# Attention into experts: routing's pieces a step later, the choice's sums on TensorE, a written order for the last four units, and the first weights around the first gather

## The chip, the cores and the metric

One core of a Trainium2 chip runs the whole program. The metric is the device time of one execution in microseconds; the time given for a kernel is the median of its runs. An execution's span runs from its first to its last instruction in the trace and is a little shorter than its time.

## What is computed

The reference, cut to what matters:

```python
# attention: 4 batches, 8 heads, 576 tokens, head size 64; fp32
scores = scale * q @ k.T + slopes * (-abs(rel))
scores = where((rel >= 0) & (rel < 128), scores, -1e9)
attn = softmax(scores)                       # each row over at most 128 keys
x = (attn @ v).reshape(2304, 512)            # 2304 tokens
# experts: 8, one per token
logits = x @ w_gate + modality_bias[modality_id]
e = argmax(logits); gate = softmax(logits)[e]
x = gate * (relu(x @ w1[e]) @ w2[e])         # 512 -> 1024 -> 512
# a dense layer
h = x @ w_in                                 # 512 -> 2048
out = (h * cos(h)) @ w_out
```

## The kernel before

**Attention.** The 2304 tokens are 18 tiles of 128 (t), in two pairs of batches (bp, nine tiles each). A unit n is one tile and one group of four heads (hg), so there are 36 units, n = 2t + hg. One step of the loop starts the scores of unit n (`score`: 12 products into bank S, then masks and the row maximum on VectorE and the exponentials on ScalarE), turns the probabilities e of unit n-2 (`flip`: transposes into bank P, a copy on ScalarE, two masks on GpSimd; units 8, 9, 26 and 27 have three key blocks and three groups of transposes, the second of them in bank T), turns q and k of a unit to come (`tr`: transposes of rqk into bank T), and forms the weighted sum of unit n-3 (`pv`: bk<-vt,pT into bank O, then den, its reciprocal and the scaling on VectorE, lines 769 to 773). Banks in this stage: S three, T two, P, O and L one each. An fp32 product is issued as two matmuls, a transpose as one.

**Routing** is woven into the same loop. When both units of a tile are summed, the tile X[t] (xt, or y for the last two) goes to `x_dram` and `later` enters its pieces under a step and a half (0 or 1) of it: `xt_split` (four transposes into bank T, a copy on ScalarE, line 803, and the rest on VectorE, line 804), and for every second tile `products` (eight products xT by wg into bank L, copied to ls), `choose` (two transposes of ls into bank L, two additions and six more operations on VectorE, the one-hot oh) and `ranks` (seven bf16 products and a dozen operations on VectorE). `setups(i)` runs setup calls twice a step: the tables all at i = 8, the modality's bias with a transpose of mf in bank T at i = 13.

**Order.** TensorE's and GpSimd's instructions keep the written order while `Turns.on` holds, from step 2 to 33; else, and on VectorE and ScalarE always, a planner orders them by its own costs. SyncE issues the loads and stores in its queue's order.

**The seam.** Tiles 0 to 15 (TE = 16) fill the first item of 256 token slots. After their ranks, `early` picks the expert with most tokens (`first`), multiplies the one-hots (`second`: ob by oa0, 16 products into bank L), gets the row indices idx0, gathers the 256 rows of `x_dram` in two halves of 128 rows (`gather(0)`, an indirect transfer issued by GpSimd into xg0 and xg1), and loads that expert's first weights: w1 in pieces of 512 KB (`load_w1`, with the expert's number read from regs by SyncE) and w2 (`load_w2`). `order` compares the experts' keys for the later plan. Behind that come the tail's units and tiles 16 and 17, whose stores stand behind the first piece of w2 (`MK["w"]`).

**Experts and after.** Nine items and the rest of 128-row blocks: each item turns its gathered rows (`to_xT`), multiplies by w1 and w2 split into two fp32r parts (casts to s on ScalarE, the rest on VectorE), and stores y. The rows of the items from the second on come from the full table (`late`: sums, slots, table on VectorE, 18 products on TensorE), which needs the ranks of tile 17. Then the dense layer, from about 435 us.

## Time and profile before

| | |
|---|---|
| median of 3 runs | 843.32 us (842.28 to 845.54) |
| the profiled execution | 844.73 us |
| its span | 843.0 us |
| TensorE busy, share of the span | 801.4 us, 95% |
| VectorE | 614.7 us, 73% |
| ScalarE | 492.1 us, 58% |
| GpSimd | 201.2 us, 24% |
| mean granted clock of TensorE | 0.989 |

How to read it: a busy time is the sum of an engine's instructions in the profiled execution; matmuls are pipelined and their ends modelled, so a following instruction may start before the shown end. The granted clock is the share of TensorE's full 2.4 GHz that the chip let through; 0.50 is 1.2 GHz. In a timeline a row is one instruction or several alike in a row, with start, time, engine, line, operation, written tile and read tiles, shapes and count; in brackets stands how long the engine was idle before it and what ended that. Lines 494 and 1079 are helpers that record many operations, so there the tile names tell them apart.

### The profile page before, as it was taken

To read this page: it belongs to the slowest core of one execution; us is meant where nothing else is said; L and a number is where in the kernel's file an instruction comes from. 1 tells how busy PE (TensorE), PEld (TensorE's weight loads), DVE (VectorE), ACT (ScalarE), POOL (GpSimd) and SP (SyncE) were. 2 spreads that over 40 slices of the span, in tenths; PEclk is the share of its full clock that TensorE was granted. 3 is DMA by queue.
4 is the path that set the end of the run, shared out by engine and by line. 5 is a ranking of instruction groups with operands and counts; after the bars stand their busy time and mean duration, and the time that the engine had idled before them with its cause. 6 is when DMAs were issued, how large, how long until landed. Compare 5 with 4: busy or idle time off the path is not lost. (4 is left out here: it accounts for less than half of the span.)

```text
span 843.0 us, 14736 instructions
## 1 busy us (share of the span) xinstructions
PE 801.4 (95%) x5269; PEld 705.8 (84%) x5269; DVE 614.7 (73%) x1463; ACT 492.1 (58%) x912; POOL 201.2 (24%) x259
## 2 busy tenths in 40 slices
PE   7899999979899999999999999999999999999996
PEld 5789888969799999999878778787788888888995
DVE  3866686668889999996749989896665555555562
ACT  6675677534557576664637676764554454444562
POOL 5655565510122132230001121112212001100100
PEclk9899999989999999999999999999999999999999
DMA  8555441044788888869433232501312001100000
GB/s 158 141 143 126 120 120 38 28 148 141 260 278 273 273 284 278 267 221 335 158 125 100 80 106 73 176 25 51 112 38 75 1 1 37 38 1 0 26 26 25
DMA packets 125134, 103.40 MB, mean 123 GB/s; under 512 B 61725, under 2 KB 105027, under 8 KB 125059
## 3 DMA queue, kind: packets, MB, share of 16 engines
q1 hardware_dynamic: 122099, 92.74, 36.3%
q0 software_dynamic: 2960, 9.70, 3.2%
q8 instruction: 42, 0.69, 0.3%
q14 instruction: 33, 0.27, 0.1%
HBM read 85.90 MB, written 16.52 MB: 121 GB/s over the span
## 5 line engine op out<-in xcount | busy, mean ns | idle before, releaser
L1079 PE MATMUL bk<-hh,s 128*128 128x256 f32 x864 | 117.7, 284 | 7.8 <-DVE y L1079 4.6
L1079 PEld LDWEIGHTS bk<-hh,s 128*128 128x128 f32 x864 | 107.8, 188 | 10.1 <-DVE y L1079 5.6
L1079 PE MATMUL bk<-xT,s 128*128 128x256 f32 x864 | 114.5, 282 | 1.7 <-DVE s L1079 1.1
L1079 POOL TENSOR_TENSOR lf<-lf,mag 128x512 f32<-128x512 f32 x32 | 46.9, 1467 | 282.1 <-DVE mag L1079 246.9
L1079 PEld LDWEIGHTS bk<-xT,s 128*128 128x128 f32 x864 | 107.4, 188 | 2.2 <-DVE s L1079 1.3
L1079 ACT CAST s<-r 128x1024 fp32r<-128x1024 f32 x72 | 75.2, 1050 | 54.4 <-DMA r<-in_moe_w_dram 40.4
L1079 PE MATMUL bk<-yT,wi_a 128*128 128x512 f32 (+1 forms) x480 | 104.4, 368 | 1.2 <-DVE yT L1079 0.8
L1079 PE MATMUL bk<-yT,wi_b 128*128 128x512 f32 (+1 forms) x480 | 105.0, 368 | 0.0
L1079 DVE TENSOR_TENSOR s<-r,s 128x1024 fp32r<-128x1024 f32 x72 | 94.3, 1313 | 13.6 <-ACT s L1079 13.2
L1079 ACT ACTIVATE r<-r 128x512 f32<-128x512 f32 (+1 forms) x80 | 47.2, 590 | 92.5 <-DVE r L1079 92.5
L1079 PEld LDWEIGHTS bk<-yT,wi_a 128*128 128x128 f32 x480 | 84.0, 188 | 17.3 <-DVE yT L1079 1.1
L1079 PEld LDWEIGHTS bk<-yT,wi_b 128*128 128x128 f32 x480 | 84.6, 188 | 15.7
L1079 DVE TENSOR_TENSOR r<-bk,r 128x512 f32<-128x512 f32 (+1 forms) x80 | 50.9, 636 | 62.1 <-ACT r L1079 61.4
L1079 PE MATMUL bk<-wo_b,gg 128*128 128x512 f32 x384 | 93.7, 391 | 2.5 <-DVE po L1079 1.1
L1079 PE MATMUL bk<-wo_a,gg 128*128 128x512 f32 x384 | 92.8, 390 | 0.6 <-DVE gg L1079 0.5
L1079 PEld LDWEIGHTS bk<-wo_b,gg 128*128 128x128 f32 x384 | 71.4, 188 | 19.7 <-ACT o L1079 1.5
L1079 PEld LDWEIGHTS bk<-wo_a,gg 128*128 128x128 f32 x384 | 71.8, 188 | 16.5 <-DVE gg L1079 1.5
L1079 DVE TENSOR_TENSOR gg<-r,gg 128x512 fp32r<-128x512 f32 x64 | 46.1, 720 | 34.3 <-ACT gg L1079 34.3
L494 PE MATMUL bk<-vt,pT 128*128 128x65 f32 x544 | 66.8, 276 | 0.1
L494 PEld LDWEIGHTS bk<-vt,pT 128*128 128x128 f32 x544 | 65.1, 195 | 1.2 <-issue 1.0
L1079 ACT CAST gg<-r 128x512 fp32r<-128x512 f32 x64 | 39.7, 620 | 41.1 <-DVE r L1079 40.2
L1079 DVE SCALAR_TENSOR_TENSOR r<-ki,bk 128x512 f32<-128x512 int32 (+1 forms) x80 | 50.4, 630 | 16.5 <-ACT ki L1079 15.9
(280 smaller groups left out, 1279.5 us busy)
## 6 DMA issues: line engine op xcount, KB each, us to landing
r<-in_moe_w_dram SPq DMA_DIRECT2D x72, 512.0 KB
y_dram<-y SPq DMA_DIRECT2D x19, 256.0 KB
rqk<-in_q_dram SPq DMA_DIRECT2D x32, 128.0 KB
rqk<-in_k_dram SPq DMA_DIRECT2D x32, 128.0 KB
vt<-in_v_dram SPq DMA_DIRECT2D x32, 128.0 KB
x_dram<-xt SPq DMA_DIRECT2D x16, 256.0 KB
f64x<-in_moe_w_in_dram SPq DMA_DIRECT2D x8, 512.0 KB
raw<-in_moe_w_dram SPq DMA_DIRECT2D x8, 512.0 KB
```

Of the source, the lines that this page charges most:

```text
L494: self.last = op(*args, **kwargs)
L1079: r = op(*args, **kwargs)
```

## The change

- `xt_split` is entered under half 1 of its step instead of half 0, `products`, `choose` and `ranks` under half 0 of the three steps behind. The calls of half 1 now come before the weighted sum.
- `choose` forms the logits in PSUM: the bias enters by a product of ident with biasm, and the two halves of ls (hi and lo weights) are summed by a product with both, a matrix of two stacked identities. The two transposes and VectorE's two additions go. The last comparison writes ohb before oh.
- The tables' setup is called one at a time from i = 8 on; `setup_route` is cut into three parts at i = 13, 14 and 15, with its transpose in bank L.
- All groups of `flip` use bank P; a weighted sum is cut after two heads, and the further groups of `flip` come in between and behind.
- The loop ends two steps sooner, and the last units' calls are written out one by one; `Turns.on` holds to the end. In this order the scaling of units 33 and 34, the masks of unit 35 and the key of `order` stand behind idx0. Sums of units 33 and 35 use bank S.
- `second` issues w1's first piece ahead of the gather; then half of the gather, a copy of the expert's number to reg0 on GpSimd, the other half, a read of reg0 on SyncE, w1's second piece and w2's first.

```diff
@@ -207,6 +207,7 @@
...
     idx = rt.tile([128, NBLK], I32, name="idx")
+    reg0 = rt.tile([1, 1], I32, name="reg0")
...
@@ -282,16 +283,22 @@
...
                 nc.tensor.matmul(tp, ob[:, t], oa0[:, t], start=t == 0, stop=t == TE - 1)
-            V_.tensor_scalar(idx0, tp, float(NT // 2), None, op0=ALU.add)
-            gather(0)
-
+            MK["idx0"] = V_.tensor_scalar(idx0, tp, float(NT // 2), None, op0=ALU.add)
             load_w1(0, 0)
+            first_rows = gather(0, 0)
+
+
+            with tc.issue_after(first_rows.ins):
+                nc.gpsimd.tensor_copy(reg0, regs[:, 2 * NL + 1:2 * NL + 2])
+            gather(0, 1)
+            EV[0] = nc.sync.value_load(reg0[0:1, 0:1], min_val=0, max_val=NE - 1)
             load_w1(0, 1)
...
             key = rt.tile([128, NE], F32, name="key")
-            V_.scalar_tensor_tensor(key, eo, -2.0 * NE, iota[:, 0:NE], op0=ALU.mult, op1=ALU.add)
+            with tc.issue_after(MK["idx0"].ins):
+                V_.scalar_tensor_tensor(key, eo, -2.0 * NE, iota[:, 0:NE], op0=ALU.mult, op1=ALU.add)
             shp = [128, NE, NE]
...
@@ -460,11 +467,13 @@
...
     def gather(i, u=None):
-        for j in range(2 if u is None else 1):
+        for j in range(2) if u is None else [u if i == 0 else 0]:
             ap = idx0[:, j:j + 1] if i == 0 else idx[:, 2 * i + j:2 * i + j + 1] if u is None else \
                 idx[:, 2 * MIN_ITEMS + u:2 * MIN_ITEMS + u + 1]
-            nc.gpsimd.indirect_dma_start(out=xgs[j], out_offset=None, in_=x_dram[0:128 * TE if i == 0 else NT, :],
-                                         in_offset=bass.IndirectOffsetOnAxis(ap=ap, axis=0))
+            ins = nc.gpsimd.indirect_dma_start(
+                out=xgs[j], out_offset=None, in_=x_dram[0:128 * TE if i == 0 else NT, :],
+                in_offset=bass.IndirectOffsetOnAxis(ap=ap, axis=0))
+        return ins
...
@@ -556,6 +565,7 @@
...
         wg = rt.tile([128, KD, 2, NE], F32R, name="wg")
+        both = rt.tile([2 * NE, NE], F32, name="both")
         wr = ca.tile([128, KD, NE], F32, name="wr")
...
@@ -576,15 +586,18 @@
...
             nc.vector.tensor_tensor(wg[:, :, 1], wr, wg[:, :, 0].bitcast(F32), op=ALU.subtract)
+            nc.vector.tensor_tensor(both, ident[:2 * NE, 0:NE], ident[:2 * NE, NE:2 * NE], op=ALU.add)
             mf = ca.tile([T, 128], F32, name="mf")
             nc.vector.tensor_copy(mf, mi.rearrange("t (p two) -> t p two", two=2)[:, :, 0])
-            mp = bank("T", [128, T])
+            yield
+            mp = bank("L", [128, T])
             nc.tensor.transpose(mp, mf, ident[:T, :T])
...
                     nc.vector.tensor_copy(md[:, 9 * bp + s:9 * bp + s + 1], mp[:, 9 * bp + 13 - s:9 * bp + 14 - s])
+            yield
             m0 = ca.tile([128, T], F32, name="m0")
...
@@ -711,6 +724,8 @@
...
                 products(sc, pairs)
+                if n == N - 1:
+                    yield
                 for j in range(2):
...
@@ -735,9 +750,9 @@
...
             for g in (0, 4, 8) if nv == 3 else (0,):
-                if g == 8:
+                if g:
                     yield
-                pp = bank("P" if g != 4 else "T", [128, 4, 128])
+                pp = bank("P", [128, 4, 128])
                 for c in range(4):
...
@@ -759,13 +774,17 @@
...
             heads, t0 = PT.pop(n)
-            ot = bank("O", [128, 4, 128])
+            ot = bank("S" if n >= END and n % 2 else "O", [128, 4, 128])
             for h, pT in enumerate(heads):
+                if h == 2:
+                    yield
                 for b in range(len(pT)):
...
             den = sm.tile([128, 4], F32, name="den")
+            if n > END:
+                yield
             nc.vector.tensor_scalar(den, ot[:, :, D], 1.0e-9, None, op0=ALU.add)
...
@@ -780,15 +799,15 @@
...
                 if t < TE - 2:
-                    later(p, 0, lambda: xt_split(t))
+                    later(p, 1, lambda: xt_split(t))
                 else:
...
                     if t < TE - 2:
-                        later(p, 1, calls[0])
-                        later(p + 1, 0, calls[1])
-                        later(p + 2, 1, calls[2])
+                        later(p + 1, 0, calls[0])
+                        later(p + 2, 0, calls[1])
+                        later(p + 3, 0, calls[2])
                     else:
...
@@ -817,25 +836,22 @@
...
             def choose():
-                lt = bank("L", [128, 2, 2, NE])
+                lg = bank("L", [128, 2, NE])
+                nc.tensor.matmul(lg, ident, biasm[:, t:t + 2], start=True, stop=False)
                 for j in range(2):
-                    nc.tensor.transpose(lt[:, j].rearrange("p a e -> p (a e)"), ls[:, 128 * j:128 * j + 128],
-                                        ident[:2 * NE, :2 * NE])
+                    nc.tensor.matmul(lg[:, j], ls[:, 128 * j:128 * j + 128], both, start=False, stop=j == 1)
                 shp = [128, 2, NE]
-                lg = rt.tile(shp, F32, name="lg")
                 mx = rt.tile([128, 2], F32, name="lmx")
...
                 rv = rev.unsqueeze(1).to_broadcast(shp)
-                nc.vector.tensor_tensor(lg, lt[:, :, 0], biasm[:, t:t + 2], op=ALU.add)
-                nc.vector.tensor_tensor(lg, lt[:, :, 1], lg, op=ALU.add)
                 nc.vector.tensor_reduce(mx, lg, op=ALU.max, axis=AX.X)
...
                 nc.vector.tensor_reduce(m2, o, op=ALU.max, axis=AX.X)
-                nc.vector.tensor_tensor(o, rv, m2.unsqueeze(2).to_broadcast(shp), op=ALU.is_equal)
-                MK["oh"] = nc.vector.tensor_tensor(ohb, rv, m2.unsqueeze(2).to_broadcast(shp), op=ALU.is_equal)
+                nc.vector.tensor_tensor(ohb, rv, m2.unsqueeze(2).to_broadcast(shp), op=ALU.is_equal)
+                MK["oh"] = nc.vector.tensor_tensor(o, rv, m2.unsqueeze(2).to_broadcast(shp), op=ALU.is_equal)
...
@@ -876,11 +892,10 @@
...
                     todo.extend(LATER.pop())
-                if i == 8:
-                    for fn in tables:
-                        fn()
-                if i == 13:
-                    setup_route()
+                if i >= 8 and tables:
+                    tables.pop(0)()
+                if i >= 13:
+                    next(route, None)
                 for fn in todo[:1 if i > 1 else 2]:
...
@@ -892,41 +907,73 @@
...
-        LATER = []
+        LATER, route = [], setup_route()
         END = N - 4
-        turned = [n + LF for n in range(N)]
-        summed = [n + LP for n in range(N)]
-        for n in range(END - 2, N):
+        turned = [n + LF for n in range(END + 1)]
+        summed = [n + LP for n in range(END)]
+        for n in range(END - 2, END + 1):
             turned[n] = max(n + 1, END)
-            summed[n] = max(n + 2, END + 1)
-        for n in range(N + 2):
+            if n < END:
+                summed[n] = END + 1
+        for n in range(END + 2):
             if n < 3:
                 ahead(n, dt=n + 1)
-            Turns.on = 1 < n <= END + 1
-            scores = score(n) if n < N else iter(())
+            Turns.on = n > 1
+            scores = score(n)
             next(scores, None)
...
             calls(due.pop((n, 0), []))
-            if n > END:
-                calls([after.pop(0) for _ in after[:2]])
-            flips = [flip(m) for m in range(N) if turned[m] == n]
+            calls(after)
+            flips = [flip(m) for m in range(END + 1) if turned[m] == n]
             for p in flips[:1]:
...
             setups(2 * n + 1)
-            sums = [m for m in range(N) if summed[m] == n]
-            for m in sums[:1]:
-                pv(m)
-            for p in flips:
+            calls(due.pop((n, 1), []))
+            sums = [pv(m) for m in range(END) if summed[m] == n]
+            for p in sums[:1]:
+                next(p)
+                for f in flips:
+                    next(f, None)
                 run(p)
-            for m in sums[1:]:
-                pv(m)
-            calls(due.pop((n, 1), []))
-            if n > END:
-                calls([after.pop(0) for _ in after[:2 if n < N + 1 else 1]])
+            for f in flips:
+                run(f)
+            for p in sums[1:]:
+                run(p)
+
+        split15, logits14, choice14, ranks14, slots0, rows0, order0 = after
+        after.clear()
+        run(score(N - 2))
+        calls(due.pop((END + 2, 0)))
         assert not due
+        split15()
+        run(flip(N - 3))
+        sum32 = pv(END)
+        next(sum32)
+        logits14()
+        run(sum32)
+        choice14()
+        score35 = score(N - 1)
+        next(score35)
+        run(flip(N - 2))
+        ranks14()
+        sum33, sum34, sum35 = (pv(n) for n in range(END + 1, N))
+        for p in (sum33, sum34):
+            next(p)
+            next(p)
+        slots0()
+        rows0()
+        with tc.issue_after(MK["idx0"].ins):
+            run(sum34)
+            run(sum33)
+            run(score35)
+        order0()
+        after.pop(0)()
+        run(flip(N - 1))
+        run(sum35)
+        after.pop(0)()
...
```

## Rows read from the trace of the kernel before

**Rows 1.** Busy time by engine, clock, DMA share and GB/s in four stretches.
```profile
core 0: us, PE busy (x) PEld busy (x) DVE busy (x) ACT busy (x) POOL busy (x), PEclk, DMA share, GB/s
20.00:160.00 140.00, 132.23 (x1232) 119.26 (x1233) 99.83 (x506) 94.78 (x242) 81.88 (x136) 0.98 0.43 106
28.00:32.00 4.00, 3.69 (x19) 3.70 (x20) 2.35 (x12) 2.72 (x8) 2.52 (x4) 0.57 0.95 221
38.00:42.00 4.00, 4.00 (x27) 3.71 (x27) 3.54 (x16) 0.92 (x2) 1.50 (x3) 0.58 0.34 101
182.00:192.00 10.00, 6.83 (x30) 4.81 (x29) 4.60 (x7) 3.70 (x6) 2.13 (x2) 0.50 1.00 349
```

**Rows 2.** Groups by form on TensorE, 20 to 178 us.
```profile
line engine op names shapes xcount | busy us, mean ns | idle before us <-releasers
L494 PE MATMUL bk<-vt,pT 128*128 128x65 f32 x528 | 64.0, 274 | 0.0
...
L494 PE MATMUL bk<-ident,rqk 128*128 128x128 f32 x116 | 18.6, 283 | 2.5 <-DVE xT L804 1.8 <-DMA rqk<-in_q_dram 0.5 <-DMA rqk<-in_k_dram 0.2
L494 PE MATMUL bk<-ident,xt 128*128 128x128 f32 x64 | 12.6, 307 | 3.6 <-DVE xt L773 3.5
L494 PE MATMUL bk<-xT,wg 128*16 128x256 f32 x64 | 9.3, 282 | 0.3 <-DVE xT L804 0.3
...
L494 PE MATMUL bk<-ident,mf 18*128 18x18 f32 x1 | 0.2, 203 | 1.3 <-DVE mf L580 1.3
```

**Rows 3.** TensorE's timeline in the loop: the longest gap that routing makes.
```profile
28.31 0.67 PE L494 MATMUL bk<-ident,xt 128*128 128x128 f32 x2 [1.70 <-DVE xt L773]
```

**Rows 4.** TensorE's timeline at the seam, 165 to 194 us.
```profile
165.94 0.97 PE L494 MATMUL bk<-kT,qT 64*128 64x256 f32 x12
166.84 0.44 PE L494 MATMUL bk<-ident,e 128*128 128x128 f32 x2
167.12 1.90 PE L494 MATMUL bk<-vt,pT 128*128 128x65 f32 x16
168.85 0.17 PE L494 MATMUL bk<-ohb,tri 128*128 128x8 bf16 x1
168.88 0.17 PE L494 MATMUL bk<-cum,ones 128*128 128x8 bf16 x1
...
181.19 0.55 PE L494 MATMUL bk<-oa,ob 128*128 128x2 f16 x16 [1.92 <-DVE oa L279]
...
188.97 1.12 PE L1079 MATMUL bk<-ident,xg 128*128 128x128 f32 x4 [2.00 <-DMA xg<-x_dram,idx]
...
190.73 1.05 PE L1079 MATMUL bk<-ident,xg 128*128 128x128 f32 x4
...
193.19 1.22 PE L1079 MATMUL bk<-xT,s 128*128 128x256 f32 x8 [0.22 <-DVE xT L1079]
```

**Rows 5.** TensorE's timeline at a choice, and what follows it.
```profile
159.29 0.29 PE L494 MATMUL bk<-ident,ls 16*128 16x16 f32 x2
159.51 0.66 PE L494 MATMUL bk<-ident,e 128*128 128x128 f32 x4
```

**Rows 6.** VectorE's timeline at the seam, 177 to 187 us.
```profile
177.85 0.16 DVE L214 TENSOR_TENSOR fold<-bk,oh 128x16 f32<-128x16 f32 x1
...
179.09 0.69 DVE L804 TENSOR_TENSOR xT<-bk,xT 128x512 fp32r<-128x512 f32 x1
...
184.52 1.23 DVE L1079 TENSOR_TENSOR s<-r,s 128x1024 fp32r<-128x1024 f32 x1
```

**Rows 7.** GpSimd's timeline: issues of the gathers, 180 to 215 us.
```profile
182.23 1.16 POOL L494 DMA_INDIRECT xg<-x_dram,idx  x1 [10.38 <-DVE idx L285]
183.69 0.97 POOL L494 DMA_INDIRECT xg<-x_dram,idx  x1 [0.30 <-issue]
209.08 1.06 POOL L1079 DMA_INDIRECT xg<-x_dram,idx  x1 [24.42 <-DVE nu L364]
```

**Rows 8.** DMA queues (packets, MB, share): first 184 to 186.5, then 187 to 189 us.
```profile
q1 hardware_dynamic: 411, 0.66, 84.9%
q0 software_dynamic: 2, 0.01, 2.3%
...
q0 software_dynamic: 143, 0.47, 59.5%
```

**Rows 9.** TensorE's timeline where the second item's rows are awaited.
```profile
212.65 0.66 PE L1079 MATMUL bk<-ident,xg 128*128 128x128 f32 x4 [0.88 <-DMA xg<-x_dram,idx]
```

## The prediction

> **What bounds the kernel now.** I began with the chain of waits and the busy shares: the chain is a chain of TensorE products from some 435 us on, and the change touches nothing there, so what it can bring is an earlier arrival at that stage. I then read TensorE's idle time stage by stage. In the attention loop, from 20 to 160 us, TensorE is busy for 132.2 of 140.0 us at a mean clock of 0.98 [rows 1]: it is the bound, and a gap in it is lost time. The groups by form say whose gaps they are: 3.5 us before the transposes of xt and 0.3 us before the logits' products, 1.8 us before the transposes of rqk (they want the bank that the token tile's split still holds, so the releaser is xT of line 804), and 1.3 us before the transposes of the modality's mf [rows 2]. All four belong to routing, 6.9 us in all. The largest, 1.70 us, ends at 28.31 [rows 3]. The granted clock in 28 to 32 us is 0.57 and in 38 to 42 us 0.58 [rows 1], so TensorE spent most of these stretches at 1.2 instead of 2.4 GHz, behind the holes of line 804's tile and of mf.
>
> The second place is the seam between attention and experts. Between 182 and 192 us the clock is 0.50 throughout, and TensorE is busy for 6.8 of 10 us even so [rows 1]. The order of TensorE's instructions shows why: the products that turn the first tokens' places into indices (oa, ob) wait 1.92 us for VectorE, then the transposes of the gathered rows wait 2.00 us for the gather, and the first expert products run freely from 193.19 [rows 4].
>
> All of this is measured in an execution that took 844.73 us (843.0 us of it the span), 1.41 us above the median of 843.32. I sum savings against 844.73 and take the same savings off the median.
>
> **The change part by part: the loop.** (a) The routing's pieces come later. The transposes of a finished tile move from right behind the scores to ahead of the weighted sum, still in the same step; logits, choice and ranks move up to one step each. The setup of the tables is cut into single calls and that of the modality into three. No work is added; 6.9 us of gaps should go. What is late next? The steps with three key blocks now put all three groups of transposes through bank P, which has one buffer, with half of a weighted sum between two groups. Sixteen products of a weighted sum take 1.73 us (167.12 to 168.85 [rows 4]), so half, of the usual size, covers 0.87 us, and a copy out of the bank has to fit into that and the transposes of rqk beside it. There are four such steps; two of them now wait for the bank of line 804, 1.8 us in all [rows 2]. I take 0.2 us each, 0.8 us in all, between 0 and 3.6.
>
> (b) The clock. The lost share is (1 - 0.57) x 4 + (1 - 0.58) x 4 = 3.4 us of full speed. If the two holes go, the work behind them runs at 2.4 GHz, and I take the 3.4 us as gained; the bounds are 0 and 3.4. Against it: 0.7 us of waiting for q and k stands in the same groups [rows 2] and stays.
>
> (c) The choice on TensorE. Two transposes become three fp32 products, and an fp32 product is issued as two matmuls here: the weighted sums count 528 for 264 [rows 2]. So six matmuls with 128 weight columns replace two instructions that take 0.22 us (159.29 to 159.51 [rows 5]). No row has fp32 matmuls with 8 or 16 moving columns. From above, an fp32 matmul of the weighted sum follows the one before it after 0.108 us (1.73 / 16 [rows 4]), with 65 columns; from below, the bf16 matmuls of the ranks, with 8 columns, follow after 0.03 us (168.85 to 168.88 [rows 4]). Type decides, I think, since the two instructions on ls, fp32 with 16 columns, also cost 0.11 each. So 6 x 0.108 = 0.65 us, 0.43 more than now. Seven rounds lie in the loop: 3.0 us lost; the bounds are a gain of 0.3 and, if each matmul costs 0.2 us, a loss of 6.9. VectorE's two additions go, but VectorE is busy for 99.8 of 140 us there [rows 1] and this saves nothing by itself. The Trainium skill (TensorE: Matmul & The Clock Gate, section Back-to-back issue gap) gives about 81 ns for a pair of weight load and matmul in a stream at 128 columns; by that the rounds would cost 1.1 us less. The trace's 0.108 us for fp32 is larger, and the measurement decides.
>
> Loop: 6.9 - 0.8 + 3.4 - 3.0 = 6.5 us.
>
> **The seam: up to the indices.** Before, the weighted sum of unit 31 ends at 168.85, after the scores of 34 and two transposes that the planner put ahead of it (1.18 us, 165.94 to 167.12); the index products begin at 181.19, 12.34 us later [rows 4]. In the written order that 1.18 us moves behind the sum. Of the 12.34 us, 1.92 was waiting; the eight transposes of tile 16 and of unit 35 move behind the index (0.14 us each by the pair at 166.84 [rows 4], 1.1 us), the 1.18 us move in, and one choice costs 0.43 more: 12.34 - 1.92 - 1.1 + 1.18 + 0.43 = 10.9 us, from a start 1.18 us sooner. Together 2.6 us sooner, if TensorE does not wait. VectorE's chain from ranks to index products ran from 177.85 to 181.19; the split that stood in it at 179.09 took 0.69 us [rows 6] and lies elsewhere in the new order; the key and its comparison, and the last units' scaling, are put behind idx0. So about 2.6 us remain of 3.3, and the weighted sums of 33 and 34 (24 matmuls, 2.6 us) stand in front of it. For the joint, and the choice's chain before it, I leave 0.4 us: 2.2 us gained. Bounds: 0.5 and 3.0.
>
> **The seam: from the indices to the first products.** Before: 181.19 to 193.19, 12.0 us. GpSimd starts the gather 1.04 us in, and the second half 1.46 us later [rows 7]. Ahead of them on SyncE's queue stood two pieces of w1, one of w2 and a store. In 184 to 186.5 us the gather's queue moved 0.01 MB and SyncE's 0.66; the gather's 0.47 MB came in 187 to 189 [rows 8], and the transposes started at 188.97, 6.74 us after the issue. A later gather with nothing ahead of it is awaited until 212.65, 3.57 us after its issue at 209.08 [rows 7, 9]. The new order issues w1's first piece, then half the gather, then a one-element copy on GpSimd, then the other half; SyncE reads that copy before it issues w1's second piece, w2's first and the stores queued behind them. The copy has no row; between 0 and the 0.97 us of a gather's issue, I take 0.4. The second half is then issued 1.04 + 1.46 + 0.4 = 2.9 us in, takes 3.6 us, and 0.7 more for sharing with w1's piece: 7.2 us. From the second half's transposes to the first products it took 2.46 us before (190.73 to 193.19): 9.7 us instead of 12.0. What hides the late second piece: issued some 3 us in, with the gather's 3.6 us and 1.5 for its half megabyte at 349 GB/s [rows 1], it lands some 8 us in; two conversions of 1.23 us [rows 6] end at 10.6, and it is wanted 24 products after the first, at about 12.3. Without that margin TensorE would wait in its place. One such conversion may fall into VectorE's routing chain, since the earlier window for it closes; I charge half, 0.6. 12.0 - 9.7 - 0.6 = 1.7 us. Bounds: -1 and 3.
>
> By the Trainium skill (DMA: Bandwidth & Descriptors, section Queues, rings and completion order) an engine takes turns between the queues that have work, packet by packet, so that a gather would not stand behind a backlog; the rows here show it standing. What follows if the rule holds all the same is rival C.
>
> **Sum.** 6.5 + 2.2 + 1.7 = 10.4 us: 834.3 in the profiled execution's terms, **832.9 us** for the median. The expert stage behind it is shifted as a whole: its weights are loaded as buffers come free, and those come free earlier too.
>
> **The rivals.**
> A. *The gaps in the loop change their name.* The transposes wait for bank P or for q and k instead of for routing, and the clock still falls. For it: q and k are awaited for 0.7 us already [rows 2]. Against it: most of a step now lies between each producer and its reader. At the upper bound of the new waits and without the clock the loop gives 6.9 - 3.6 - 3.0 = 0.3, and with the seam's 3.9 that is 4.2: 839.1.
> B. *The written tail makes the last tile late.* The last unit's masks, exponentials, transposes and sum now all follow idx0, on four engines in turn, at half the clock. If products of tile 17 end 2.5 us later than I reckon, ranks and the full table are late, and the second item waits for its tokens, as it already does for 0.88 us at 212.65 [rows 9]. The second part of the seam then loses 1 us instead of gaining 1.7: 6.5 + 2.2 - 1.0 = 7.7: 835.6.
> C. *Holding back w1 buys nothing*, because the gather's delay was not the backlog. The second part of the seam gives 0: 8.7 saved, 834.6. Against it: the gather's packets came only when SyncE's queue thinned out [rows 8]. By the rule of the Trainium skill cited above (DMA: Bandwidth & Descriptors) this would be the outcome.
> D. *Slower: the choice opens holes.* Each of its six matmuls shows its whole latency, 274 ns as the mean of such a one [rows 2], because each adds to the same bank: 1.64 us instead of 0.22, and a hole of that size was followed by a stretch at the low clock that cost 1.7 us [rows 1, 3]. Seven rounds cost 7 x (1.42 + 1.7) = 21.8; against 6.1 of gaps, 3.4 of clock and 1.5 left of the seam, 10.8 slower: 854.1. It decides from about 1.6 us a round, hole and clock together. Against it: the weighted sums add to one bank too and follow at 0.108 us.
>
> **How the numbers follow.** A measurement of this kernel can tell about 0.5%, 4.2 us, from no change. Forecast 0.46, all faster. A 0.18, which straddles that bound: 0.07 faster, 0.11 within. B 0.13: 0.08 and 0.05. C 0.10: 0.09 and 0.01. D 0.13, slower. Together 0.70, 0.17, 0.13. The low end takes the cheap bound of the choice and no new waits: 832.9 - 3.3 - 0.8 - 1.8 = 827.0. The high end is A with the choice at 0.2 us a matmul, 3.9 more, 843.0, of which I leave out the last bit: 842.5. D stands outside.
>
> **What would show it.** Right: no gap before xt, mf and rqk beyond 22 to 25 us; clock 1.00 from 26 to 180 us; six matmuls per choice some 0.65 us long; the index products near 172.5; the first half of the gather some 3.6 us after its issue; the first expert products near 183, and the same stage behind them, shifted whole. Wrong: gaps before e, or clock below 1 in the loop (A); a later ranks of tile 17 and a longer wait at the second item's gather (B); the gather still 6 to 7 us (C); holes around the choice (D). A shift of the start that is given back before 435 us would show a bound in the expert stage that I have not priced.

## The result: slower, and where the time went

The changed kernel takes 852.61 us (median of 4 runs, 850.94 to 853.65), the kernel before beside it 843.87 (842.28 to 845.54): a ratio of 1.0088 with the interval [1.0065, 1.0112]. Here and below ratio and interval are those on record; the ratio leaves out the few runs far above the rest and is not the quotient of the two medians (1.0104 here). The forecast was 832.9 with a range up to 842.5: the change went the other way. The profiled execution took 852.2 us, its span is 850.5.

First the windows, for the stretches of [rows 1] and two new ones, with the same columns.

```profile
core 0: us, PE busy (x) PEld busy (x) DVE busy (x) ACT busy (x) POOL busy (x), PEclk, DMA share, GB/s
20.00:160.00 140.00, 134.59 (x1273) 121.23 (x1271) 96.62 (x504) 95.93 (x248) 82.20 (x138) 1.00 0.43 107
28.00:32.00 4.00, 3.85 (x38) 3.68 (x39) 1.10 (x7) 3.29 (x10) 3.68 (x7) 1.00 0.96 218
38.00:42.00 4.00, 2.77 (x23) 1.97 (x23) 3.76 (x22) 2.48 (x7) 2.67 (x5) 1.00 0.92 207
166.00:174.00 8.00, 7.01 (x45) 6.70 (x46) 4.05 (x26) 1.66 (x6) 1.22 (x2) 0.57 0.08 33
182.00:192.00 10.00, 6.76 (x40) 4.79 (x37) 6.24 (x24) 5.03 (x9) 2.33 (x3) 0.61 0.83 265
408.00:416.00 8.00, 5.64 (x26) 5.64 (x27) 6.20 (x9) 3.83 (x8) 0.00 (x0) 0.60 0.37 102
```

The loop looks as forecast at first sight: the clock is 1.00 and the two low stretches are gone (e4 below shows how far that is due to the change). But TensorE is still idle for 5.4 of 140 us (before 7.8), and busy for 2.4 us more. The groups by form on TensorE, 20 to 160 us, say with what, and who makes the gaps now. Compare [rows 2], which run on to 178 us; up to 160 us the gaps before xt, rqk, mf and wg are the same there.

```profile
line engine op names shapes xcount | busy us, mean ns | idle before us <-releasers
L503 PE MATMUL bk<-ident,e 128*128 128x128 f32 x153 | 24.5, 282 | 1.7 <-ACT pT L760 0.9 <-ACT pa L760 0.8
L503 PE MATMUL bk<-ident,rqk 128*128 128x128 f32 x116 | 17.7, 273 | 0.9 <-DMA rqk<-in_q_dram 0.7 <-DMA rqk<-in_k_dram 0.2
L503 PE MATMUL bk<-ident,xt 128*128 128x128 f32 x56 | 8.7, 276 | 0.3 <-DVE xt L792 0.3
L503 PE MATMUL bk<-xT,wg 128*16 128x256 f32 x56 | 8.7, 282 | 1.9 <-DVE xT L823 1.0 <-ACT xT L822 0.7
L503 PE MATMUL bk<-both,ls 16*128 16x8 f32 x24 | 3.6, 256 | 0.0
L503 PE MATMUL bk<-biasm,ident 128*128 128x16 f32 x12 | 2.4, 273 | 0.0
L503 PE MATMUL bk<-ident,mf 18*128 18x18 f32 x1 | 0.2, 231 | 0.0
```

The gap before xt fell from 3.5 to 0.3 and that before mf is gone. In their place stand the copies out of bank P (pT, and pa where a unit has two key blocks: 1.7, before e) and the logits' products (1.9, before 0.3). The two groups with 24 and 12 matmuls are the choice, six rounds of it. TensorE's timeline shows a round, the joint to the written tail, and the seam:

```profile
161.37 0.98 PE L503 MATMUL bk<-kT,qT 64*128 64x256 f32 x12
162.28 0.40 PE L503 MATMUL bk<-biasm,ident 128*128 128x16 f32 x2
162.60 0.61 PE L503 MATMUL bk<-both,ls 16*128 16x8 f32 x4
163.14 0.66 PE L503 MATMUL bk<-ident,xt 128*128 128x128 f32 x4
...
166.99 3.47 PE L503 MATMUL bk<-vt,pT 128*128 128x65 f32 x16 [1.02 <-DVE xt L792]
...
181.73 0.54 PE L503 MATMUL bk<-oa,ob 128*128 128x2 f16 x16
...
183.93 0.44 PE L503 MATMUL bk<-ident,y 128*128 128x128 f32 x2 [1.38 <-DVE y L792]
184.20 1.27 PE L503 MATMUL bk<-ident,e 128*128 128x128 f32 x4
186.14 1.97 PE L503 MATMUL bk<-vt,pT 128*128 128x65 f32 x8 [0.68 <-ACT pT L760]
...
191.23 1.05 PE L1126 MATMUL bk<-ident,xg 128*128 128x128 f32 x4
...
195.98 0.51 PE L1126 MATMUL bk<-xT,s 128*128 128x256 f32 x2 [1.06 <-ACT xT L1126]
196.71 0.62 PE L1126 MATMUL bk<-xT,s 128*128 128x256 f32 x3 [0.21 <-DVE xT L1126]
```

A round of the choice takes 162.28 to 163.14, 0.86 us, against 0.22 [rows 5]. Unit 31's sum (166.99) waits 1.02 us for bank O, which unit 30's sum holds until it is scaled (xt, line 792); before, unit 34's scores stood there [rows 4]. Behind the wait the clock falls and the sum takes 3.47 us instead of 1.90. Behind the indices (181.73) stands unit 35's chain with two waits, then the gathered rows, which are there when their turn comes. Against the kernel before, the changed one stands like this ("run freely" is the first expert product behind which the stage's start has no more waits):

| us | before | after | |
|---|---|---|---|
| scores of unit 33 | 162.28 | 161.37 | -0.91 |
| index products | 181.19 | 181.73 | +0.54 |
| expert products run freely | 193.19 | 196.71 | +3.52 |
| second item's rows turned | 212.65 | 216.98 | +4.33 |
| first item-end wait past 400 us | 405.04 | 410.36 | +5.32 |
| dense layer | 435.68 | 444.02 | +8.34 |

The forecast had -6.5 in the first row, -8.7 in the second, -10.4 from the third on. The last two rows are a second stage that I had not priced. The timeline there, of the kernel before and then of the changed one:

```profile
401.15 2.00 ACT L1079 CAST s<-r 128x1024 fp32r<-128x1024 f32 x2 [4.43 <-DMA r<-in_moe_w_dram]
405.04 3.11 PE L1079 MATMUL bk<-hh,s 128*128 128x256 f32 x24 [1.48 <-ACT y L1079]
```

```profile
406.48 1.99 ACT L1126 CAST s<-r 128x1024 fp32r<-128x1024 f32 x2 [6.12 <-DMA r<-in_moe_w_dram]
410.36 5.49 PE L1126 MATMUL bk<-hh,s 128*128 128x256 f32 x24 [3.15 <-ACT y L1126]
```

ScalarE's row comes first in each, TensorE's second. The copies of y that free the accumulators stand on ScalarE behind casts that wait for weights. TensorE waits 3.15 us instead of 1.48, and the clock is 0.60 in 408 to 416 us: 5.49 us for 24 matmuls that took 3.11.

### The profile page after: what moved, and what is told of

Its sections match the earlier page's. It is cut to its first block, busy times and chain, and to the rows that moved or that the text cites. A ratio compares the mean times of both kernels' runs of the same rounds, so it can differ in the third digit from the quotient of the medians.

```text
span 850.5 us, 14784 instructions
## 1 busy us (share of the span) xinstructions
PE 811.6 (95%) x5305; PEld 716.2 (84%) x5305; DVE 610.1 (72%) x1446; ACT 491.7 (58%) x912; POOL 200.9 (24%) x260
## 5 line engine op out<-in xcount | busy, mean ns | idle before, releaser
L1126 PE MATMUL bk<-hh,s 128*128 128x256 f32 x864 | 119.9, 287 | 8.0 <-DVE y L1126 4.0
L1126 PE MATMUL bk<-xT,s 128*128 128x256 f32 x864 | 116.4, 285 | 2.4 <-DVE s L1126 1.1
L1126 PEld LDWEIGHTS bk<-hh,s 128*128 128x128 f32 x864 | 110.2, 192 | 10.0 <-DVE y L1126 5.2
L743 ACT ACTIVATE e<-sx,nm 128x128 f32<-128x128 f32 (+1 forms) x144 | 51.0, 418 | 25.2 <-DVE nm L740 24.8
```

Of the source, the lines that this page charges most:

```text
L743: MARK["act"] = nc.scalar.activation(e[:, h, :wv], x[:, :wv], AF.Exp, bias=nm[:, h:h + 1], scale=-1.0)
L1126: r = op(*args, **kwargs)
```

## The experiments

Medians are over all runs of a kernel, ratios to the kernel before beside it, with their interval. Executions of one kernel differ in the clock they are granted: over 105 runs of the kernel before, the time falls by 0.58 us for each 0.001 of mean granted clock (correlation -0.81; 839.16 to 852.72 us). So I read places from a trace, and what an edit is worth from the medians. Below, "the line" is this straight line of time over clock: a kernel's distance from it is its time against the kernel before at equal clock. One trace is one execution: e6's is the fastest of its ten runs (840.36 us), e7's the slowest (846.12).

### One edit at a time

e1 is the kernel before with the new `choose` alone, e2 with the later pieces of routing alone (due times, setups, one bank for all turned groups), e4 with the split gather and held-back w1 alone. e3 is the changed kernel with the planner's order of the last four units back; e5 is the changed kernel with the old `choose`.

> The kernel before, with the choice alone changed: the logits' sum and bias formed by TensorE's products in PSUM. If the choice's price is what the trace after shows (0.86 us from its first matmul to the next work, against 0.22 before, so 0.64 us in each of seven rounds of the loop and two at the seam), 848 to 850 us. If the price hides in gaps that the old loop has anyhow, 844 to 845.

> Only the routing's pieces a step later, the setup cut up, and the order of flips and sums in a step; choice, tail and first weights as before. If routing's gaps and the low clock behind them were lost time and go, 6 to 8 us faster than before: 836 to 838. If the gaps only change their name (waits for ScalarE's copies and the tile's split, as the trace after shows 4 us of them), 0 to 3 us faster: 841 to 844.

> The changed kernel with the planner's order of the last four units put back. If the written order makes the seam's loss (bank O's wait at unit 31's sum, the low clock behind it, unit 35 behind the index), the seam's 4.4 us and what follows from them at 405 us go: 842 to 846. If choice or first weights make it, it stays at 850 to 853.

> The kernel before, with only w1's second piece put behind half of the gather. If the gather lands sooner and the weights' delay is covered, 0 to 2 us faster: 842 to 844. If the delayed weights come back as the late wait for y behind the casts near 405 us, 3 to 5 us slower: 847 to 849.

> The changed kernel with the choice put back on VectorE; routing's later pieces, the written tail and the split gather stay. Theory: the choice on TensorE is the largest loss. It cost 3.75 us by unit 33 and some 7 us in the whole when it was the only edit. Without it the scores of unit 33 begin near 157 to 158 us, the index products near 178, and the time is 844 to 847 us. Rival: the written tail and the held-back piece lose by themselves as much as the choice does; then the scores of unit 33 are early as well, but the first expert products still run after 194 us and the time stays at 849 us or more.

| | median us | ratio | unit 33 | index products | free products | second item |
|---|---|---|---|---|---|---|
| e1 choice | 852.84 | 1.0084 [1.0051, 1.0116] | 166.03 | 185.25 | 198.49 | 219.11 |
| e2 later pieces | 844.97 | 0.9972 [0.9939, 1.0004] | 158.81 | 178.68 | 190.66 | 211.86 |
| e3 planner's tail | 851.27 | 1.0052 [1.0019, 1.0085] | 160.72 | 183.60 | 195.22 | 217.57 |
| e4 gather | 846.66 | 1.0015 [0.9982, 1.0047] | 159.54 | 178.45 | 191.60 | 212.17 |
| e5 no choice | 845.43 | 0.9995 [0.9968, 1.0023] | 161.27 | 178.61 | 192.23 | 213.24 |

The choice alone loses as much as the whole change, and taking it out of the change gives that back: e1 and e5 agree on 7 to 8 us. The later pieces gain 0.8 us on the median, and the interval does not exclude nothing; the gather alone gains nothing; the planner's tail does not repair the change. e1 lies above both numbers expected of it, e5 within its theory (though its unit 33 starts late: that execution ran at 0.91 in 20 to 60 us), e2, e3 and e4 in or near their rivals' ranges: the later pieces gain little, and neither the written tail nor a late piece that TensorE itself waits for is the main loss. e4's rival had the delayed weights come back near 405 us; there TensorE waits 1.51 us in e4's trace (1.48 before), so they do not.

The columns from unit 33 on hold the clock of one execution as well as the edit. e4 leaves the loop as it was, with 8.1 us of idle time from 20 to 160 us (7.8 before). Its gaps at the places of the two low stretches are 1.11 us (1.70 before) and 1.19 (1.27). Still its clock is 1.00 there, and its unit 33 starts 2.74 us sooner than in the trace of the kernel before. Its rows, with the columns of [rows 1] in the two windows:

```profile
28.28 0.44 PE L502 MATMUL bk<-ident,xt 128*128 128x128 f32 x2 [1.11 <-DVE xt L781]
34.45 0.20 PE L502 MATMUL bk<-ident,mf 18*128 18x18 f32 x1 [1.19 <-ACT e L736]
30.00:32.00 2.00, 2.00 (x24) 1.93 (x23) 0.90 (x4) 2.00 (x7) 1.13 (x2) 1.00 1.01 223
38.00:40.00 2.00, 1.92 (x18) 1.92 (x18) 2.00 (x12) 1.44 (x4) 0.33 (x2) 1.00 0.44 147
```

### Why the gather alone gained nothing

The timeline of e4, three rows of ScalarE and the wait that they make on TensorE:

```profile
188.04 1.04 ACT L1087 CAST s<-r 128x1024 fp32r<-128x1024 f32 x1 [4.79 <-DMA r<-in_moe_w_dram]
189.00 0.58 ACT L1087 CAST xT<-bk 128x512 fp32r<-128x512 f32 x1
189.47 0.36 ACT L1087 COPY ls<-bk 16x256 f32<-16x256 f32 x1
189.88 0.39 PE L1087 MATMUL bk<-ident,ls 16*128 16x16 f32 x2 [2.98 <-ACT ls L1087]
```

The rows were turned at 184.14, but the cast of w1's late piece stood first in ScalarE's queue and waited 4.79 us, with the cast of those rows and of ls behind it. e6 puts it behind; e7 adds the later pieces to that (no choice on TensorE, planner's tail).

```
-        split_w1(0, 1)
+        with tc.issue_after(xt[0].ins):
+            split_w1(0, 1)
```

> The kernel before with the split gather and the held-back piece of w1, and one edit more: the conversion of that piece is issued on ScalarE behind the cast of the gathered rows' second half. Theory: the split gather gained nothing by itself because that conversion, first in ScalarE's queue, waited 4.79 us for its weights with the casts of xT and of ls behind it. Behind the cast it keeps nobody waiting, the first expert products run near 187 us instead of 190.4, and the time is 841 to 844 us. Rival: TensorE would have waited for that late piece anyway, or the weights bound the expert stage; then the first products come sooner, a wait for the piece's conversion appears within 10 us behind them, the second item's gather is turned near 212 us as before, and the time is 845 to 848 us.

> The kernel before with routing's pieces a step later, the split gather and the gated conversion, but with the choice on VectorE and the planner's order of the tail. Theory: the gains add: about 2.5 us at the index products, and about 3 us from the gather; 837 to 841 us. Rival: the expert stage takes its time from the weights that are loaded for it, so what comes sooner waits longer at the end of an item or near 405 us; then the second item's gather is turned 3 us or more ahead of the kernel before, the dense layer starts within 1 us of 435.7, and the time is 842 to 846 us.

TensorE in e6:

```profile
178.76 0.55 PE L502 MATMUL bk<-oa,ob 128*128 128x2 f16 x16 [1.92 <-DVE oa L280]
...
184.45 1.06 PE L1087 MATMUL bk<-ident,xg 128*128 128x128 f32 x4
...
187.89 4.51 PE L1087 MATMUL bk<-xT,s 128*128 128x256 f32 x17 [0.35 <-ACT xT L1087]
```

From the indices to free products it is now 9.13 us (12.0 before; 9.37 in e7, to 188.22), and TensorE doesn't wait for the gather (0.19 us in e7): the local mechanism holds. The median does not follow. e6 has 846.03, 1.0012 [0.9974, 1.0050]. e7 has 842.67, 0.9963 [0.9933, 0.9994]: the one version whose whole interval lies below the kernel before, by 2.8 us under it on the median (845.45 beside it). Both times lie in the rivals' ranges. In e7's trace the second item's rows are turned at 208.88, 3.8 us sooner, but SyncE issues that item's weights at 208.99 instead of 211.61, 2.6 sooner; by the code it must first read the expert's number out of the routing table. TensorE then waits 2.41 us at 214.30 for their conversion, and the clock is 0.71 in 210 to 220 us. That is how the slowest of e7's ten runs lost its lead; e6's trace, the fastest of its ten, has no such wait and turns the second item's rows at 210.44, 2.2 us sooner. So the second item's start is a place where a lead can go, but that it takes the lead in the median run is not shown.

### The bank behind unit 30, and the tail

e8 is the changed kernel with unit 31's sum in a bank of the scores. e11 adds the old `choose` and e6's edit.

```
-            ot = bank("S" if n >= END and n % 2 else "O", [128, 4, 128])
+            ot = bank("S" if n >= END - 1 and n % 2 else "O", [128, 4, 128])
```

> The changed kernel with one edit: the weighted sum of unit 31 takes a bank of the scores instead of the one bank that unit 30's sum holds. Theory: the 1.02 us wait for that bank ahead of the sum of unit 31 starts the stretch at the low clock behind it, in which the sum took 3.47 instead of 1.90 us. Without it the index products start some 2.5 to 3.5 us sooner, near 178.5, the first expert products some 3 us sooner, and the time is 848 to 850.5 us. Rival: the clock falls there anyway, because the chain behind it has gaps of its own; then the index products start at most 1 us sooner and the time is 851 to 853 us.

> The changed kernel with three edits: the choice back on VectorE, the weighted sum of unit 31 in a bank of the scores, the conversion of w1's second piece behind the cast of the gathered rows. If the gains add, 845.4 of the kernel without the choice less some 3.3 for the bank: 840 to 843 us, below the kernel before. Rival: the weights of the second item wait for the routing table in any case, so that what comes sooner at the first products waits there: 844 to 846 us.

e8 takes 849.28, 1.0043 [1.0011, 1.0075], against 1.0088 [1.0065, 1.0112] with the wait: index products at 178.43 instead of 181.73, both as the theory said. The median gains more than the 1.02 us of the wait itself. Is the rest the fall of the clock behind it? e5 has the wait without the choice, e8 the choice without the wait. TensorE's timeline of e5, then of e8:

```profile
166.24 1.97 PE L503 MATMUL bk<-vt,pT 128*128 128x65 f32 x16 [1.02 <-DVE oh L854]
```

```profile
164.12 3.69 PE L503 MATMUL bk<-vt,pT 128*128 128x65 f32 x32
167.73 0.98 PE L503 MATMUL bk<-kT,qT 64*128 64x256 f32 x12
```

In both the sum takes its usual 1.8 to 2.0 us for 16, at full clock. Of these three traces only the one with both the choice's small products at 162.28 and the wait at 166 fell. But each is one execution, and e3 speaks against a rule: its order has no wait of TensorE between 160 and 182 us, and behind the next choice the clock falls all the same, to 0.71 in 174 to 176 us and 0.50 in 176 to 184. TensorE in e3:

```profile
173.93 0.29 PE L503 MATMUL bk<-biasm,ident 128*128 128x16 f32 x2
174.15 0.61 PE L503 MATMUL bk<-both,ls 16*128 16x8 f32 x4
...
175.27 3.52 PE L503 MATMUL bk<-vt,pT 128*128 128x65 f32 x16
```

e1, with the same choice at 177.81, stays at 1.00 up to 184 us. That the other bank removes the wait is shown; that the wait brought the clock down is not.

e11 takes 843.93, 0.9978 [0.9952, 1.0004]. Its index products come at 175.14, 6.05 sooner than before, but free products only 15.3 us later: unit 35's chain (1.39 and 0.68 us of waits) stands ahead of the gathered rows, and then TensorE waits 2.84 us for their cast, which ScalarE holds behind the absolute value (mag) of some of the dense layer's weights. That instruction waits 2.28 us for its DMA. Of the lead 1.1 us are left at the second item (211.58). The time falls between theory and rival.

### What the choice costs, and where

e9 has the choice on TensorE in the loop's seven rounds only, e10 in the two rounds of the seam only; in e12 TensorE sums the logits' parts and VectorE adds the bias.

```
+            choose = choose_pe if t < TE - 2 else choose_ve   (e9; e10: t >= TE - 2)
...
-                nc.tensor.matmul(lg, ident, biasm[:, t:t + 2], start=True, stop=False)   (e12)
+                nc.vector.tensor_tensor(lg, ps, biasm[:, t:t + 2], op=ALU.add)
```

> The kernel before with the choice on TensorE in the seven rounds of the attention loop only; the last two rounds, in the seam, stay on VectorE. All nine rounds cost 7.1 us. Theory: the price is paid per round on TensorE, which bounds the loop: seven rounds at 0.54 us, 3.75 us by unit 33, and little more behind it: 848 to 850.5 us. Rival: the seven rounds are covered in large part by gaps that the loop has anyway, and the last two rounds, which stand in the chain that ends last at half the clock, cost the most: 845 to 847 us.

> The kernel before with the choice on TensorE in the last two rounds only, those of the seam. By the theory of a price per round, twice some 1.3 us at half the clock at the most: 846 to 848 us, and no more than 3 of the 7.1 us. By the rival, in which the chain of the seam is the place of the loss, 848 to 851 us: the index products or the first expert products come 3 us or more later than before.

> The kernel before with half of the choice on TensorE in all nine rounds: the two products that sum the logits' parts stay there, the bias is added on VectorE. In the rows of the changed kernel these products take 0.54 us in place of 0.22, the product with the bias another 0.32. Theory, price by TensorE's instructions: 0.32 dearer a round instead of 0.64, half of the loss: 847.5 to 850 us. Rival: it is the chain through TensorE's bank and the accumulation that costs, not the number of matmuls: either all of the loss stays, 850.5 to 854 us, or none, 844 to 846.5 us.

e9: 856.31, 1.0107 [1.0072, 1.0143]. e10: 848.92, 1.0030 [0.9998, 1.0063]. e12: 851.14, 1.0058 [1.0024, 1.0092]. Loop and seam stand as more than three to one, so most of it is paid in the loop. e10's 3.0 us are in the rival's range, but its unit 33, ahead of its edit, was already 1.76 late at a clock of 0.91 in 100 to 120 us; from there to the free products it lost 1.6. Half of the choice (e12) costs two thirds of the loss: the median is in the range of the rival that kept all of it, and the interval also allows the half of the theory. e9 is above its theory, above even e1, which does more, so the two parts do not add up to the whole. The two ran on different chips, each beside the kernel before, and e9's profiled execution ran at 0.72 in 20 to 40 us, ahead of any choice, where e1's ran at 0.88. Set against the line, e9 lies 7.7 us above it, e1 6.4, e12 4.1, e10 1.0.

Is it the choice's own chain, or only TensorE's time? e13 keeps the old choice and adds to each of the seven rounds four fp32 products that nobody reads; e14 puts all 28 into the last of these rounds.

```
+                for j in range(4 if t < TE - 2 else 0):                  (e14: 28 if t == TE - 4 else 0)
+                    nc.tensor.matmul(lt[:, 2, j % 2], ls[:, 128 * (j % 2):128 * (j % 2) + 128], ident[:2 * NE, :NE],
+                                     start=True, stop=True)
```

> The kernel before, choice on VectorE, and in each of the loop's seven rounds four more fp32 products of the choice's shape that nobody reads, behind the two transposes: eight matmuls, by the rows of the changed kernel 0.135 us each, 1.08 us a round, 7.6 us in all. Theory: only TensorE's time counts, and a later start of the expert stage grows on the way to the dense layer as it did with the choice (3.75 us at unit 33, 7 in the end): 854 to 859 us. Rival: a delay of the loop is carried through one to one, and the choice lost the rest through its own chain (bank, accumulation, the last rounds): 851.5 to 853.5 us, with the dense layer no later against before than the scores of unit 33.

> The same 28 unused products, all in one place, in the loop's last round near unit 30: 56 matmuls, some 7.6 us there. Theory, a later expert stage is what grows: the loss is 9 us or more, as in the kernel with four products a round, 854 to 859 us. Rival: what grows is the disturbance of each step, not the delay: 851.5 to 853.5 us here, and more with four products in each round.

TensorE in e13, where two transposes and eight added matmuls take 1.11 us (44.41 to 45.52), 0.11 for each added one:

```profile
44.41 1.18 PE L494 MATMUL bk<-ident,ls 16*128 16x16 f32 x10
45.52 0.65 PE L494 MATMUL bk<-ident,e 128*128 128x128 f32 x4
```

e13: 855.49, 1.0095 [1.0057, 1.0133], inside its theory's range. Seven times 0.89 is 6.2 us of work; unit 33 is 4.6 later, the second item 6.8, the span 10.8, the median 8.7. The choice's seven rounds add 4.5 us of work (0.64 each) and cost 7.1 us (e1, with the seam's two) to 10.4 (e9). So products without a reader lose about as much, and the chain (accumulation, bank) isn't needed to explain the loss; that it adds nothing is not shown. The loss grows on the way: the gather is awaited 3.00 us instead of 2.00, and the clock is 0.85 in 200 to 210 us. e14 took 861.56, 1.0181 [1.0136, 1.0226], more than either theory, for a reason of its own. Its timeline at the added products, and the windows around them:

```profile
159.33 10.56 PE L494 MATMUL bk<-ident,ls 16*128 16x16 f32 x58
```

```profile
core 0: us, PE busy (x) PEld busy (x) DVE busy (x) ACT busy (x) POOL busy (x), PEclk, DMA share, GB/s
158.00:160.00 2.00, 2.00 (x24) 1.63 (x21) 0.99 (x3) 0.36 (x1) 1.82 (x3) 1.00 0.00 0
160.00:162.00 2.00, 2.00 (x17) 2.00 (x16) 1.03 (x9) 1.28 (x4) 0.00 (x0) 0.83 0.03 8
162.00:164.00 2.00, 2.00 (x12) 2.00 (x11) 0.00 (x0) 0.00 (x0) 0.00 (x0) 0.50 0.00 0
...
176.00:178.00 2.00, 2.00 (x15) 1.78 (x12) 1.29 (x7) 0.24 (x1) 1.09 (x2) 0.50 0.32 124
178.00:180.00 2.00, 2.00 (x18) 2.00 (x17) 1.00 (x5) 1.68 (x5) 0.68 (x2) 0.90 0.00 0
```

TensorE is busy for 2.00 of 2.00 us, and the clock falls to 0.50 all the same. The six runs bear the trace out: their mean clock is 0.975, that of the kernel before beside them 0.983. So 56 small matmuls cost 10.3 us instead of 6.2, and the work behind them up to 178 us runs at half speed. From the free products on its delay grows little (15.1 us there, 16.8 at the second item's rows, 17.2 in the span). In e13 it grows from 5.1 to 10.8, in e1 from 5.3 to 8.0, in e12 from 3.1 to 6.1. That a delay grows behind the loop is therefore seen, but not by a fixed share; which of gather, clock and weights carries it was not taken apart.

## Point by point: where the prediction went wrong

The forecast was 10.4 us faster, 13.4 of gains less 3.0 for the choice; measured is 8.7 us slower by the medians. Two steps failed. The choice was priced at 3.0 us and costs 7 to 8 (e1, e5). And the gains do not reach the median: without the choice the change is worth nothing that can be told from zero (e5, 0.9995).

**Routing's gaps (6.9 less 0.8 of new waits).** Wrong, and it was the first half of rival A; the clock, its other half, did not fall. The gaps named in [rows 2] went, but the loop's idle time in e2 is 7.9 us (before 7.8). In 20 to 160 us it is the ranks waiting for ohb (1.9), the logits' products for xT (1.9), e for pT and pa (2.1), rqk mostly for q and k (1.8). Two of these groups in e2:

```profile
L496 PE MATMUL bk<-ident,e 128*128 128x128 f32 x152 | 24.1, 281 | 2.1 <-ACT pT L751 1.3 <-ACT pa L751 0.8
...
L496 PE MATMUL bk<-ohb,tri 128*128 128x8 bf16 x12 | 1.4, 173 | 1.9 <-DVE ohb L846 1.9
```

I priced only the pT copy as a new wait. The step that failed is "most of a step now lies between each producer and its reader". My reading, which no run isolates: with the gaps gone TensorE reaches every reader sooner, while VectorE and ScalarE are no faster.

**The clock (3.4).** The size is that of the trace, but the cause was half wrong. In e2 and in the changed kernel the clock is 1.00 from 20 to 160 us, and unit 33 is 3.47 us sooner in e2 with no less idle time, so all of that is clock. Yet e4, with the old loop and its gaps, is at 1.00 there too: the low stretches of [rows 1] belong to that execution and not to the order alone, and "if the two holes go" is no condition for the 3.4 us. What the later pieces do is seen only over many runs: the mean clock is 0.987 to 0.988 in e2, e7, e8 and e11, but 0.985 in e5 and 0.984 in e3, which have them too; it is 0.984 in the kernel before, 0.982 and 0.984 in e4 and e6. By the line e2's gain in clock is worth some 2 us, an estimate, and at equal clock e2 is no quicker (1.2 us above the line). It isn't certain in each execution, as e5 shows. The first low stretch also followed the gap that line 773 ended [rows 3], not line 804's.

**The choice (-3.0).** Right mechanism, too small, and not followed to the end. A round is 0.64 us dearer, not 0.43: the product with the bias takes 0.16 for a matmul and the sums 0.135, against 0.108. In e13's uniform stream they take 0.11, near my figure; the choice changes its weights' shape between products, which may be the rest, and no run isolates it. The Trainium skill (TensorE: Matmul & The Clock Gate, section Back-to-back issue gap) has about 81 ns for a pair in a stream, which fits neither. By unit 33 seven rounds cost 3.75 us (e1), near the forecast; by the end 7. Of the two rounds behind the loop the sum priced one, at 0.43; in e1's trace the delay grows from 3.75 us at unit 33 to 5.3 at the free products. Beyond that "The expert stage behind it is shifted as a whole" is the sentence that failed: in e1 the late start met a clock of 0.87 in 200 to 210 us (1.00 before) and a wait of 2.65 us past 400 instead of 1.48, in e13 also a longer wait for the gather.

**Up to the indices (2.2).** The sum was right, the cover was not. From unit 33's scores to the index products it was 18.9 us before, and 16.4 in e11 and 17.0 in e8, a gain of 2.5 and 1.9; in the changed kernel it is 20.4, and between it and e8 only the bank of unit 31's sum differs. Of those 3.4 us 1.02 are the wait; the rest comes with the low clock of that execution. I wrote "if TensorE does not wait" and did not ask what unit 31's sum would be queued behind once unit 34's scores moved away: a bank with one buffer, released by the scaling of the unit just before it.

**From the indices to the first products (1.7).** Right for the gather, wrong for the rest. GpSimd's copy takes 0.18 us (0.4 assumed) and the gathered rows are hardly awaited, so rival C, and with it the rule of the Trainium skill that queues take turns (DMA: Bandwidth & Descriptors, section Queues, rings and completion order), gets no support from e4, e6 and e7: in e4 the first rows were turned 4.6 us after the gather's issue with nobody waiting for them, before 6.74. With e6's edit the stretch is 9.13 us where the sum's 9.7 (without the half conversion) stood. Two things were missed. TensorE's wait for the late piece was priced, but not what stands behind its cast on ScalarE (e4). And rival B was the case and worse than priced: with unit 35's chain ahead of the rows the stretch is 15.0 us in the changed kernel, 15.3 in e11 and 13.6 in e5.

**The rivals' bounds.** D, the slower side, rested on holes around the choice. There are none; its sign came true by another way, through a price per matmul inside what I had bounded (up to 6.9 us lost), added to gains that did not come. Nor was the fast side sound: its last term, 1.8 us, names no row, and the seam's two upper bounds would give 2.1.

## What to carry to other kernels

A gap on the bounding engine is worth its length only if what its next instructions read is also early: after taking a gap out of a sum, list the next producer for each instruction that moves up. On an engine that is busy for 94% of a stretch, six small matmuls in place of two instructions cost their whole time, and moving two additions to it from an engine with room to spare is a loss. When work is reordered, walk each in-order queue and each single-buffered bank past the new place and write down what now stands directly behind what.

## What the hardware showed that I had not expected

TensorE's clock fell to 0.50 while the profile shows the engine busy all the time, with small fp32 products in a row, 16 rows of weights by 8 columns (0.50 is 1.2 of 2.4 GHz; e14, 162 to 178 us; the ends of matmuls are modelled). The Trainium skill (TensorE: Matmul & The Clock Gate, section What's actually happening) says that activity releases the throttle and that the clock follows how busy the engine was. Going by the busy time in these rows it should have stayed up; the trace does not agree, and the measurement decides. The same wait of 1.02 us was followed by 0.50 where the choice stood shortly ahead of it, and by 1.00 where it did not (e5), in one execution each; in e3 the clock fell behind a choice without a wait.

The same instructions in the same order can meet another clock: 20 to 40 us, ahead of any edit that could matter there, shows 0.88 before, 0.88 in e1, 1.00 in e4 and 0.72 in e9. One profile of this kernel says where that execution's time went; with ten to twelve runs the interval is still some 3 us to either side, so an edit of 3 us is only just told from nothing (e7, e8).
